# Sums of weight blocks: two of four by accumulating DMAs in place of VectorE

## The chip, the cores and the metric

The kernel runs on one core of one Trainium2 chip. The metric is the device time of one execution in microseconds (us); before the change the median of three runs is 703.41 us (703.22 to 703.43). All trace times below count from the start of the profiled span.

## The reference

One transformer layer on 2048 tokens of width 448, in float32:

```python
h  = x + fnet(layernorm(x))          # fnet: Real(DFT over tokens of DFT over width)
h2 = h + geglu(layernorm(h))         # (gelu(xn @ w_gate) * (xn @ w_up)) @ w_down, inner width 1792

# fnet:
a = einsum("bsd,ed->bse", x, dft_hid_re);  b = einsum("bsd,ed->bse", x, dft_hid_im)
y = einsum("ts,bse->bte", dft_seq_re, a) - einsum("ts,bse->bte", dft_seq_im, b)
```

The DFT matrices are inputs: those over tokens, 2048 x 2048 real and imaginary, are together the large operand W of the first stage.

## The kernel before, in words

The kernel applies W to the normalised x first (the sequence stage, to about 340 us) and the small DFT over the width after it, row block by row block. Gate, up and down projections follow. Every float32 operand is split into a high and a low float16 part (`hi_part`, L108, on ScalarE; `lo_part`, L112 and L114, on VectorE), and every product is three matmuls: high by high, high by low, low by high (`TERMS`).

The sequence stage is a loop over 64 units of W, `for n in range(N_STEPS)`. A unit is eight blocks of 128 x 128. Units 0 to 39 are multiplied block by block (`seq_mm`, L637). From unit `FAST` = 40 on, four units make one pass that uses products of Strassen's kind: for each pair of 2 x 2 blocks seven products (`PRODUCTS`) in place of eight. They need, beside the raw blocks A11, A12 and A22, four sums of the unit's blocks, S1 to S4 (`FORMS`), and sums of x's halves (T1 to T4, made by `t_load`, `t_norm`, `t_sums`, `t_hi` and `t_lo`). The matmuls are `fast_mm` (L509), 42 to a unit: two inner blocks i, seven products, three terms. A pass's seven sums in PSUM are combined by `fast_out` (L538, L541) into `zs`, which DMA transposes turn (`z_turn`, L658); the products with the small DFT are `hid_mm` (L719).

A unit n from 40 on goes through these steps:

- `seq_load(n)`: two DMAs on SP's queue (L421), one for each i, bring four blocks each (2 KB a partition) into the tile `wr`.
- `fast_sums(n)`: VectorE writes the four sums into a tile `sums`. L460 makes two of them in one instruction (blocks 1 and 2, each plus block 3, 512 elements a partition), L461 and L462 one each of 256 elements.
- `fast_raw(n)`: high and low part of the three raw blocks (768 elements).
- `fast_split(n)`: high part of the sums, two instructions of 512 elements on ScalarE, and low part, one instruction of 1024 elements on VectorE.
- `fast_mm(n, ...)`: the matmuls.

The order is written out by hand: each engine runs its instructions in the order of the program text, and SP its DMAs likewise. At step n, unit n is multiplied while unit n + 2 is prepared; after `fast_split` of unit n + 2 the load of unit n + 4 is issued. `fast_at` holds the steps of the first units (36, 38, 39, then 41 on). In the last unit of each pass (n % 4 == 3) `fast_raw` and `fast_split` come between the pieces of `fast_out`. The lists `early` and `after` place the other work of a step: loads, transposes, stores and splits of the gate and up weights (`Weights`), layer norm sums, hidden products. All DMAs are issued by SP; POOL does nothing between 1.4 us and 337.8 us.

`wr` and `sums` share a ring of five slots (tag `wr`); a slot is given out again when its tile's last reader is done, the one that came free first being the next. The inputs of `t_sums` lie in another ring, tag `xt`, of three slots.

Of the kernel before, what the change touches and what calls it, by code (L numbers as in the profile page):

```python
# [9 lines left out]
F32 = mybir.dt.float32  # L10
AF = mybir.ActivationFunctionType
ALU = mybir.AluOpType

P = 128
# [12 lines left out]
D_SC = 64.0  # L27
# [5 lines left out]
def kernel(  # L33
# [39 lines left out]
    nc = tc.nc  # L73
    V, A, G, PE = nc.vector, nc.scalar, nc.gpsimd, nc.tensor
# [32 lines left out]
    def hi_part(dst, src, scale=1.0):  # L107
        A.activation(dst, src, AF.Copy, scale=scale)  # L108

    def lo_part(dst, src, hi, scale=1.0):  # L110
        if isinstance(scale, float) and scale == 1.0:
            V.tensor_sub(dst, src, hi)  # L112
        else:
            V.scalar_tensor_tensor(dst, src, scale, hi, op0=ALU.mult, op1=ALU.subtract)  # L114
# [187 lines left out]
    dft = seq.enter_context(tc.tile_pool(name="dft", bufs=1, side="right"))  # L302
# [51 lines left out]
    xt, xs, norm_x = {}, {}, {}  # L354
# [51 lines left out]
    wr, ws = {}, {}  # L406

    def step_of(n):

        k, qq = divmod(n - NT, 4)  # L410
        return 2 + k // 2, k % 2, qq

    def seq_load(n):
        wr[n] = dft.tile([P, 8 * P], F32, tag="wr", bufs=5, name=f"wr{n}")
        if n < NT:
            nc.sync.dma_start(wr[n].rearrange("p (b t) -> p b t", b=4), w_seq[8 * (n % 2) + n // 2])
            return
        p, part, qq = step_of(n)
        for i in range(2):
            dst = wr[n][:, i * 4 * P : (i + 1) * 4 * P].rearrange("p (g t) -> p g t", g=2)  # L420
            nc.sync.dma_start(dst, w_seq[8 * p + 2 * qq + i][:, 2 * part : 2 * part + 2, :])  # L421
# [19 lines left out]
    FAST = N_STEPS - 24  # L441
    A_RAW = ("A12", "A11", "A22")
    FORMS = ("S3", "S1", "S2", "S4")
    T_OPS = ("T1", "T3", "T4", "T2")
    PRODUCTS = ("A11", "B11"), ("A12", "B21"), ("S2", "T2"), ("S3", "T3"), ("S1", "T1"), ("S4", "B22"), ("A22", "T4")
    fast_w, fast_s, fast_t, fast_acc, fast_e = {}, {}, {}, {}, {}

    def fast_views(n):
        raw = wr[n].rearrange("p (i b t) -> p i b t", i=2, b=4)
        s = fast_s[n].rearrange("p (s i t) -> p s i t", s=4, i=2)  # L450
        src = raw[:, :, 0:3].rearrange("p i b t -> p i (b t)")
        dst = fast_w[n][0][:, :, : 6 * P].rearrange("p l (i b) -> p l i b", i=2)
        return raw, s, src, dst

    def fast_sums(n):
        fast_s[n] = dft.tile([P, 8 * P], F32, tag="wr", bufs=5, name=f"sums{n}")
        fast_w[n] = [fast_tile(n, k, **place) for k, place in enumerate(fast_places(n))]
        raw, s, src, dst = fast_views(n)
        by_block = raw.rearrange("p i b t -> p b i t")
        V.tensor_add(s[:, 0:2], by_block[:, 1:3], by_block[:, 3:4].to_broadcast([P, 2, 2, P]))  # L460
        V.tensor_add(s[:, 2], s[:, 1], raw[:, :, 1])  # L461
        V.tensor_add(s[:, 3], raw[:, :, 0], s[:, 2])  # L462

    def fast_tile(n, k, pool=None, **place):
        return (pool or dft).tile([P, 2, 8 * P], F16, **place, name=f"ws{n}_{k}")

    def fast_places(n):
        ring = dict(tag="ws", bufs=6)
        return (dict(tag="raw", bufs=2, pool=prep), ring) if n == FAST + 2 else (ring, ring)

    def fast_raw(n):

        raw, s, src, dst = fast_views(n)
        hi_part(dst[:, 0], src, D_SC)
        lo_part(dst[:, 1], src, dst[:, 0], D_SC)

    def fast_split(n):

        w = fast_w[n][1]
        for part in slice(0, 4 * P), slice(4 * P, 8 * P):  # L480
            hi_part(w[:, 0, part], fast_s[n][:, part], D_SC)
        lo_part(w[:, 1], fast_s[n], w[:, 0], D_SC)

    def fast_a(n, i, l, name):
        if name in FORMS:
            k = 2 * FORMS.index(name) + i
            return fast_w[n][1][:, l, k * P : (k + 1) * P]
        k = 3 * i + A_RAW.index(name)
        return fast_w[n][0][:, l, k * P : (k + 1) * P]
# [14 lines left out]
    def fast_mm(n, i, k):  # L504

        j = 2 * (n % 4) + i
        a, b = PRODUCTS[k]
        for m, (lw, lx) in enumerate(TERMS):
            PE.matmul(  # L509
                fast_sum(n, k),  # L510
                fast_a(n, i, lw, a),
                fast_b(j, lx, b),
                start=j == 0 and m == 0 and k % 2 == 0,
                stop=j == NT // 2 - 1 and m == 2,
                skip_group_check=True,
            )
# [249 lines left out]
    for p, (n, half) in enumerate(turns):  # L766
        b, j = divmod(p, 2)
# [39 lines left out]
    for n in range(2, 5):  # L807
        seq_load(n)
# [27 lines left out]
    for n in range(N_STEPS):  # L836
# [10 lines left out]
        if n + 3 < FAST:  # L847
            seq_load(n + 5)
# [13 lines left out]
        if n in fast_at:  # L862
            unit = fast_at.index(n) + FAST
            fast_sums(unit)

            if n < FAST or n % 4 < 3:
                fast_raw(unit)
                fast_split(unit)
                if unit + 2 < N_STEPS:
                    seq_load(unit + 2)  # L870
# [7 lines left out]
        if n >= FAST:  # L878

            last = n % 4 == 3  # L880
            one = [(i, k) for k in range(7) for i in range(2)] if last else [(i, k) for i in range(2) for k in range(7)]
            if n % 4 == 0 and n > FAST:

                ks = (4, 5, 2, 3, 0, 1) if n == N_STEPS - 4 else range(6)
                one = [(i, k) for i in range(2) for k in ks] + [(i, 6) for i in range(2)]
            for m, (i, k) in enumerate(one):
                fast_mm(n, i, k)
                if last and i == 1 and k in (1, 3, 5, 6):  # L890
                    fast_out(n, k)
                    if n < N_STEPS - 1:
                        unit = n + 2
                        if k == 1:
                            fast_raw(unit)
                        elif k == 3:
                            fast_split(unit)
                            if unit + 2 < N_STEPS:
                                seq_load(unit + 2)
                if m in (6, 13):  # L900
                    for what in after.get((n, m // 7), ()):
                        what()
            continue
# [11 lines left out]
        else:  # L915
            p, part, qq = step_of(n)
# [392 lines left out]
    for t in range(NF):  # L1309
        w = gu.get(t + 2) if t + 2 in JIT_F else None  # L1310
        n = PREP_AT.get(t)
# [90 lines left out]
    for t in range(NF, N_GU):  # L1402
        now, ahead = steps[t], steps.get(t + 1, [])
# [36 lines left out]
        if ends:  # L1440
            p = now[-1] // NC
# [21 lines left out]
        for p, t0 in ended.items():  # L1463
            each = 3 if p < 3 else 2
            n = each * (t - t0)
# [106 lines left out]
```

## Time and profile before

| | |
|---|---|
| Median of three runs | 703.41 us |
| Profiled execution: its time, its span | 703.2 us, 701.1 us |
| TensorE busy | 696.3 us (99% of the span), clock 1.00 |
| VectorE, ScalarE, POOL busy | 551.0, 400.0, 95.4 us |
| Matmuls of the seven-product passes (L509) | from 219.2 to 339.9 us, 1008 of them |
| VectorE's sums, L460, L461, L462 | 24 times 684, 425 and 425 ns (medians) |
| DMA | 161.29 MB, queue of SP 76.0% of 16 engines |

The profile lists, for each engine, how long it was busy, and for each group of instructions its source line, what it writes and reads, its count, its busy time and what ended the idle time before it. The chain of waits follows the last instruction back through whatever released it; a stage in which the chain is all TensorE without gaps is one in which nothing made TensorE wait. The trace also gives single instructions in order of time (start, duration, engine, line), and busy times in stretches of the span.

### The profile page before, as it was taken

Reading aid. Unit: us, or ns where it says so; the run is one execution under the profiler, and the core shown is the slowest. Engines: PE = TensorE matmul, PEld = TensorE weight load, DVE = VectorE, ACT = ScalarE, POOL = GpSimd, SP = SyncE. Lnnn points to the kernel's source line nnn. Section 1 sums busy time; section 2 is a strip of 40 time slices with the busy share of each in tenths; the row PEclk is TensorE's granted clock in tenths of the full one; section 3 lists DMA queues with packets and bytes.
Section 4 is the critical chain, followed back from the end, with each engine's and each line's share of the span. In section 5 each row is a group of like instructions: output and inputs, shape, how many; then the busy total and the mean of one; then the engine's idle time right before and its main releaser. Section 6 shows DMA issues by size and latency. Waiting matters only on the chain.

```text
span 701.1 us, 13638 instructions
## 1 busy us (share of the span) xinstructions
PE 696.3 (99%) x5164; PEld 500.6 (71%) x5164; DVE 551.0 (79%) x1187; ACT 400.0 (57%) x787; POOL 95.4 (14%) x88
## 2 busy tenths in 40 slices
PE   9999999999999999999999999999999999999998
PEld 5555555555557889997644444469999999999997
DVE  7998667786798999986547798767777867899786
ACT  5876556666676566564526666555555453655631
POOL 0000000000000000000223333311020111232224
PEclk9999999999999999999999999999999999999999
DMA  8798578999997487384836878797879985877612
GB/s 276 252 255 303 121 267 227 334 288 289 269 287 195 141 195 200 117 205 179 233 125 212 288 242 236 189 326 231 245 209 326 247 299 170 318 274 276 239 39 79
DMA packets 116321, 161.29 MB, mean 230 GB/s; under 512 B 61984, under 2 KB 80544, under 8 KB 116256
## 3 DMA queue, kind: packets, MB, share of 16 engines
q1 hardware_dynamic: 116256, 160.43, 76.0%
q8 instruction: 40, 0.66, 0.4%
q14 instruction: 25, 0.20, 0.1%
HBM read 112.16 MB, written 34.34 MB: 209 GB/s over the span
## 4 chain that ended last, share of the span: by engine, by line
PE 98%; issue 1%; DMA 0%; DVE 0%; ACT 0%
PE acc L637 26%; PE acc_d L1232 15%; PE pY L1028 15%; PE acc_f L509 14%; PE pZ L1028 10%; PE pX L1028 10%; PE y L719 9%; DMA x<-in_x_dram 0%; ACT dn_w L108 0%; ACT v L958 0%; DVE st_x L122 0%; DVE xs L149 0%; DVE hr L1508 0%; ACT sd_x L129 0%; DVE r_x L373 0%
## 5 line engine op out<-in xcount | busy, mean ns | idle before, releaser
L637 PE MATMUL acc<-xs,ws 128*128 128x448 f16 x960 | 183.1, 352 | 0.1
L1028 PEld LDWEIGHTS <-gw 128*128 128x128 f16 x1443 | 140.9, 98 | 51.6
L637 PEld LDWEIGHTS <-ws 128*128 128x128 f16 x960 | 93.9, 98 | 87.7 <-DVE ws L114 0.2
L1232 PE MATMUL acc_d<-wd,dn_w 128*128 128x224 f16 x1008 | 110.6, 259 | 0.0
L1232 PEld LDWEIGHTS <-dn_w 128*128 128x128 f16 x1008 | 97.0, 98 | 1.9
L1028 PE MATMUL pY<-hops,gw 128*128 128x256 f16 (+1 forms) x629 | 98.1, 298 | 0.0
L509 PEld LDWEIGHTS <-ws 128*128 128x128 f16 x1008 | 96.6, 98 | 1.3
L1122 POOL TENSOR_TENSOR hs<-hs,c 128x256 f32<-128x256 f32 (+1 forms) x42 | 59.5, 1417 | 247.6 <-ACT c L1120 185.3
L114 DVE SCALAR_TENSOR_TENSOR ws<-wr,ws 128x1024 f16<-128x1024 f32 (+2 forms) x66 | 72.0, 1092 | 20.8 <-ACT ws L108 16.3
L108 ACT ACTIVATE ws<-wr 128x1024 f16<-128x1024 f32 (+2 forms) x66 | 61.9, 941 | 13.4 <-DMA wr<-in_w_seq_dram 8.0
L509 PE MATMUL acc_f<-t,ws 128*128 128x224 f16 x576 | 68.2, 259 | 0.0
L1028 PE MATMUL pZ<-hops,gw 128*128 128x256 f16 (+1 forms) x407 | 67.1, 298 | 0.0
L1028 PE MATMUL pX<-hops,gw 128*128 128x256 f16 (+1 forms) x407 | 67.1, 298 | 0.0
L719 PE MATMUL y<-wh,z 128*128 128x448 f16 x336 | 66.2, 352 | 0.0
L1073 ACT ACTIVATE pY<-pX 128x256 f32<-128x256 f32 (+1 forms) x42 | 18.4, 439 | 66.3 <-PE pX L1028 63.0
L215 POOL TENSOR_TENSOR wd_s<-wd 128x448 f32<-128x448 f32 x7 | 9.7, 1390 | 337.1 <-DVE e L538 336.3
L509 PE MATMUL acc_f<-xs,ws 128*128 128x224 f16 x432 | 55.1, 259 | 0.0
L719 PEld LDWEIGHTS <-z 128*128 128x128 f16 x336 | 32.9, 98 | 29.7
L1038 DVE SCALAR_TENSOR_TENSOR c<-pZ,u 128x256 f32<-128x256 f32 (+1 forms) x42 | 21.4, 510 | 38.8 <-PE pZ L1028 22.8
L1084 ACT ACTIVATE u<-pY 128x256 f32<-128x256 f32 (+1 forms) x42 | 19.1, 454 | 53.5 <-PE pY L1028 53.4
L112 DVE TENSOR_TENSOR dn_w<-dn_s,dn_w 128x640 f16<-128x640 f32 x48 | 41.5, 865 | 1.5 <-ACT dn_w L108 1.4
L108 ACT ACTIVATE dn_w<-dn_s 128x640 f16<-128x640 f32 x48 | 34.9, 728 | 12.1 <-DVE dn_s L1194 12.0
(144 smaller groups left out, 909.5 us busy)
## 6 DMA issues: line engine op xcount, KB each, us to landing
gw<-w_dram SPq DMA_DIRECT2D x37, 896.0 KB, 6.5
wr<-in_w_seq_dram SPq DMA_DIRECT2D x100, 256.0 KB, 4.6
hid_dram<-hs SPq DMA_DIRECT2D x27, 512.0 KB, 5.9
hid<-hid_dram SPq DMA_DIRECT2D x54, 256.0 KB, 5.8
w_dram<-gu_w SPq DMA_DIRECT2D x14, 896.0 KB, 6.5
gu_raw<-in_w_gu_dram SPq DMA_DIRECT2D x28, 384.0 KB, 6.1
wr<-in_w_seq_dram SPq DMA_DIRECT2D x14, 512.0 KB, 5.2
x<-in_x_dram SPq DMA_DIRECT2D x16, 224.0 KB, 3.1
```

The lines of the kernel that those rows point to most:

```text
L108: A.activation(dst, src, AF.Copy, scale=scale)
L112: V.tensor_sub(dst, src, hi)
L114: V.scalar_tensor_tensor(dst, src, scale, hi, op0=ALU.mult, op1=ALU.subtract)
L509: PE.matmul(fast_sum(n, k), fast_a(n, i, lw, a), fast_b(j, lx, b), start=j == 0 and m == 0 and k % 2 == 0, stop=j == NT // 2 - 1 and m == ...
L637: PE.matmul(acc[key][:, :D], w[:, lw, block * P : (block + 1) * P], xs[c][:, lx, :], start=c == 0 and m == 0, stop=c == NT - 1 and m == 2,)
L719: PE.matmul(y[:, :D], z[p][:, lz, k, g * P : (g + 1) * P], wh[:, lw, k, :], start=p == NP - 1 and k == 0 and m == 0, stop=k == 6 and m == ...
L1028: PE.matmul(ps, w[:, wl, wa + ws, :], ops[:, m + ms, :], start=first and n == 0, stop=last and n == len(terms) - 1, skip_group_check=True,)
L1038: V.scalar_tensor_tensor(dst, ps, SC, other, op0=ALU.mult, op1=ALU.add)
L1073: A.activation(self.Y, self.X, AF.Copy)
L1084: A.activation(self.u2, self.Y, AF.Copy, scale=SC)
L1122: G.tensor_mul(c22, c22, self.cols(self.c12))
L1232: PE.matmul(ps, w[:, la, a, :], wd[n][:, lb, b, :], start=n == 0 and m == 0 and opens, stop=n == NC - 1 and m == 2, skip_group_check=True,)
```

## The change

For units from 40 on the load is a function of its own. W's tile holds three raw blocks for each i in place of four. Beside it a tile of the same ring, shared by two units, receives blocks 1 and 2 by two plain DMAs on SP; then two DMAs issued by POOL add block 3, read from DRAM twice over by a broadcast access pattern, onto both. These two sums are thus ready when the second pair of DMAs has landed. `fast_sums` makes the other two on VectorE, 256 elements each, into a tile of the ring `xt`. `fast_split` and `fast_a` follow the new layout: the low part of the sums is two instructions of 512 elements.

```diff
     def seq_load(n):
+        if n >= FAST:
+            fast_load(n)
+            return
...
+    def fast_load(n):
+        p, part, qq = step_of(n)
+        wr[n] = dft.tile([P, 2, 3 * P], F32, tag="wr", bufs=5, name=f"wr{n}")
+        if n % 2 == 0:
+            pair["now"] = dft.tile([P, 2, 2, 2, P], F32, tag="wr", bufs=5, name=f"sums{n}")
+        fast_s[n] = pair["now"][:, n % 2]
+        blocks = [w_seq[8 * p + 2 * qq + i].rearrange("p g t -> p (g t)")[:, 4 * part * P :] for i in range(2)]
+        for i in range(2):
+            nc.sync.dma_start(fast_s[n][:, i], blocks[i][:, P : 3 * P].rearrange("p (s t) -> p s t", s=2))
+        for i in range(2):
+            nc.sync.dma_start(wr[n][:, i], blocks[i][:, 0 : 3 * P])
+        for i in range(2):
+            G.dma_start(
+                fast_s[n][:, i],
+                blocks[i][:, None, 3 * P : 4 * P].to_broadcast([P, 2, P]),
+                accum_op=ALU.add,
+            )
...
     def fast_sums(n):
-        fast_s[n] = dft.tile([P, 8 * P], F32, tag="wr", bufs=5, name=f"sums{n}")
         fast_w[n] = [fast_tile(n, k, **place) for k, place in enumerate(fast_places(n))]
-        raw, s, src, dst = fast_views(n)
-        by_block = raw.rearrange("p i b t -> p b i t")
-        V.tensor_add(s[:, 0:2], by_block[:, 1:3], by_block[:, 3:4].to_broadcast([P, 2, 2, P]))
-        V.tensor_add(s[:, 2], s[:, 1], raw[:, :, 1])
-        V.tensor_add(s[:, 3], raw[:, :, 0], s[:, 2])
+        t = dft.tile([P, 2, 2, P], F32, tag="xt", bufs=3, name=f"more{n}")
+        raw, sa = fast_views(n)[0], fast_s[n]
+        fast_s[n] = sa, t
+        V.tensor_add(t[:, :, 0], sa[:, :, 1], raw[:, :, 1])
+        V.tensor_add(t[:, :, 1], raw[:, :, 0], t[:, :, 0])
...
     def fast_split(n):
 
-        w = fast_w[n][1]
-        for part in slice(0, 4 * P), slice(4 * P, 8 * P):
-            hi_part(w[:, 0, part], fast_s[n][:, part], D_SC)
-        lo_part(w[:, 1], fast_s[n], w[:, 0], D_SC)
+        w = fast_w[n][1].rearrange("p l (h i s t) -> p l h i s t", h=2, i=2, s=2)
+        for h in range(2):
+            hi_part(w[:, 0, h], fast_s[n][h], D_SC)
+        for h in range(2):
+            lo_part(w[:, 1, h], fast_s[n][h], w[:, 0, h], D_SC)
```

More of the change, by code (lines that the diff above doesn't have):

```diff
@@ L445 @@
     PRODUCTS = ("A11", "B11"), ("A12", "B21"), ("S2", "T2"), ("S3", "T3"), ("S1", "T1"), ("S4", "B22"), ("A22", "T4")
-    fast_w, fast_s, fast_t, fast_acc, fast_e = {}, {}, {}, {}, {}
+    fast_w, fast_s, fast_t, fast_acc, fast_e, pair = {}, {}, {}, {}, {}, {}
+    def fast_load(n):
[15 more added lines that the diff above has]
+            )
     def fast_views(n):
-        raw = wr[n].rearrange("p (i b t) -> p i b t", i=2, b=4)
-        s = fast_s[n].rearrange("p (s i t) -> p s i t", s=4, i=2)
-        src = raw[:, :, 0:3].rearrange("p i b t -> p i (b t)")
+        src = wr[n]
+        raw = src.rearrange("p i (b t) -> p i b t", b=3)
         dst = fast_w[n][0][:, :, : 6 * P].rearrange("p l (i b) -> p l i b", i=2)
-        return raw, s, src, dst
+        return raw, src, dst
     def fast_sums(n):
-        fast_s[n] = dft.tile([P, 8 * P], F32, tag="wr", bufs=5, name=f"sums{n}")
         fast_w[n] = [fast_tile(n, k, **place) for k, place in enumerate(fast_places(n))]
-        raw, s, src, dst = fast_views(n)
-        by_block = raw.rearrange("p i b t -> p b i t")
-        V.tensor_add(s[:, 0:2], by_block[:, 1:3], by_block[:, 3:4].to_broadcast([P, 2, 2, P]))
-        V.tensor_add(s[:, 2], s[:, 1], raw[:, :, 1])
-        V.tensor_add(s[:, 3], raw[:, :, 0], s[:, 2])
+        t = dft.tile([P, 2, 2, P], F32, tag="xt", bufs=3, name=f"more{n}")
[3 more added lines that the diff above has]
+        V.tensor_add(t[:, :, 1], raw[:, :, 0], t[:, :, 0])
     def fast_tile(n, k, pool=None, **place):
@@ L471, in fast_raw @@
     def fast_raw(n):
-        raw, s, src, dst = fast_views(n)
+        raw, src, dst = fast_views(n)
         hi_part(dst[:, 0], src, D_SC)
@@ L477, in fast_split @@
     def fast_split(n):
-        w = fast_w[n][1]
-        for part in slice(0, 4 * P), slice(4 * P, 8 * P):
-            hi_part(w[:, 0, part], fast_s[n][:, part], D_SC)
-        lo_part(w[:, 1], fast_s[n], w[:, 0], D_SC)
+        w = fast_w[n][1].rearrange("p l (h i s t) -> p l h i s t", h=2, i=2, s=2)
[3 more added lines that the diff above has]
+            lo_part(w[:, 1, h], fast_s[n][h], w[:, 0, h], D_SC)
     def fast_a(n, i, l, name):
         if name in FORMS:
-            k = 2 * FORMS.index(name) + i
+            f = FORMS.index(name)
+            k = f // 2 * 4 + 2 * i + f % 2
             return fast_w[n][1][:, l, k * P : (k + 1) * P]
```

## The prediction

> **What bounds the kernel now.** I read the page's parts 1 and 4 first, then the chain of waits in order of time over the stage of the change, then that stage in windows of 20 us.
>
> ```profile
> span 701.1 us, 13638 instructions
> ...
> PE 696.3 (99%) x5164; PEld 500.6 (71%) x5164; DVE 551.0 (79%) x1187; ACT 400.0 (57%) x787; POOL 95.4 (14%) x88
> ...
> PE 98%; issue 1%; DMA 0%; DVE 0%; ACT 0%
> ```
> ```profile
> 219.40 18.11 PE acc_f L509 x189
> 237.51 3.97 PE y L719 x21
> ...
> 331.79 8.05 PE acc_f L509 x84
> ```
> ```profile
> 219.00:240.00 21.00, 21.00 (x207) 19.58 (x204) 19.35 (x43) 11.57 (x21) 0.00 (x0) 1.00 0.71 182
> 240.00:260.00 20.00, 20.00 (x190) 18.15 (x189) 19.61 (x37) 12.88 (x25) 0.00 (x0) 1.00 0.68 147
> 260.00:280.00 20.00, 20.00 (x191) 18.10 (x189) 19.49 (x39) 12.86 (x25) 0.00 (x0) 1.00 0.79 206
> 280.00:300.00 20.00, 20.00 (x190) 18.11 (x189) 18.59 (x31) 11.57 (x22) 0.00 (x0) 1.00 0.39 129
> 300.00:320.00 20.00, 20.00 (x191) 18.14 (x189) 17.61 (x30) 10.92 (x21) 0.00 (x0) 1.00 0.75 195
> 320.00:340.00 20.00, 20.00 (x181) 17.14 (x180) 9.69 (x25) 8.95 (x21) 2.19 (x3) 1.00 0.64 223
> ```
>
> The windows give length, then busy time of PE, PEld, DVE, ACT and POOL, granted clock, DMA share, GB/s. TensorE is busy throughout the stage at a clock of 1.00. A matmul of a seven-product pass takes 18.11 / 189 = 0.0958 us, a unit of 42 takes 4.02 us. 24 units (96.6 us) and six groups of 21 for L719 (6 x 3.97 = 23.8 us) make 120.4 us, and the stage lasts from 219.40 to 331.79 + 8.05 = 339.84, also 120.4 us. So not one microsecond in it is a wait of TensorE. VectorE, at 19.35 to 19.61 us of 20 up to 280 us, is nearly full too, but nothing on the chain waits for it.
>
> **What the change takes from VectorE.**
>
> ```profile
> 233.46 0.69 DVE L460 TENSOR_TENSOR sums<-wr 128x512 f32<-128x512 f32 x1 [0.93 <-DMA wr<-in_w_seq_dram]
> 234.19 0.43 DVE L461 TENSOR_TENSOR sums<-sums,wr 128x256 f32<-128x256 f32 x1
> 234.65 0.43 DVE L462 TENSOR_TENSOR sums<-wr,sums 128x256 f32<-128x256 f32 x1
> 234.99 0.42 DVE L243 TENSOR_TENSOR tt<-xn_h 128x256 f32<-128x256 f32 x1
> ...
> 238.36 1.22 DVE L114 SCALAR_TENSOR_TENSOR ws<-sums,ws 128x1024 f16<-128x1024 f32 x1
> 239.49 1.40 DVE L538 SCALAR_TENSOR_TENSOR e<-acc_f,e 128x224 f32<-128x224 f32 x4
> ```
> ```profile
> L114 DVE SCALAR_TENSOR_TENSOR ws<-wr,ws x66: 681/1218/1227, 5.8 to 324.9; 128x1024 f16<-128x1024 f32 x38, 128x768 f16<-128x768 f32 x24, 128x512 f16<-128x512 f32 x4
> ```
>
> From start to start the three sums of a unit hold VectorE 234.99 - 233.46 = 1.53 us. What stays is two adds of 256 elements, 234.99 - 234.19 = 0.80 us: 0.73 us less. The low part of the sums becomes two instructions of 512 in place of one of 1024: the one holds the engine 239.49 - 238.36 = 1.13 us; one of 512 takes 0.681 us in the last row, some 0.6 from start to start, so the two take 0.07 more. Net 0.66 us a unit, 15.8 us over 24 units. On the path this is worth nothing: TensorE, busy 20.00 of 20.00 us, hides it. ScalarE's high parts keep their forms, two of 512 a unit.
>
> **What it adds.** A unit's two loads on SP become four (the two for the sums first), and two DMAs on POOL follow that wait for the sums' loads. VectorE's first add, which wanted a landed load only, now wants a landed accumulation. Behind the POOL waits stands nothing: POOL's own list of waits has one of 336 us there.
>
> ```profile
> POOL wd_s L215 <- DVE e L538: 336.3, 1, 336.3
> ```
>
> So the question is when the accumulations land, and which unit has the least room. Most units' loads lie many microseconds ahead of use; unit 45 (L460 at 233.46 above) is the one that already waited 0.93 us for its load, because its load stands on SP behind a store that waits for VectorE and behind four transposes:
>
> ```profile
> 220.73 0.33 SPq L351 DMA_DIRECT2D w_dram<-gu_w  x1
> 221.15 7.51 SPq L658 DMA_TRANSPOSE z<-zs  x4
> ```
> ```profile
> 228.70 2.01 SPq L421 DMA_DIRECT2D wr<-in_w_seq_dram  x4
> ```
>
> The room from there to TensorE: a unit's first matmuls on sums are its third product. In units 46, 47 and 48 those start at
>
> ```profile
> 247.94 1.03 PE L509 MATMUL acc_f<-t,ws 128*128 128x224 f16 x9
> ...
> 252.53 1.89 PE L509 MATMUL acc_f<-t,ws 128*128 128x224 f16 x18
> ...
> 255.99 1.03 PE L509 MATMUL acc_f<-t,ws 128*128 128x224 f16 x9
> ```
>
> and the third matmul of each, 0.19 us later, is the first that reads the low part. Below, the start of unit 46's sums, and the low part of each of the three:
>
> ```profile
> 242.08 0.69 DVE L460 TENSOR_TENSOR sums<-wr 128x512 f32<-128x512 f32 x1
> ...
> 244.47 1.22 DVE L114 SCALAR_TENSOR_TENSOR ws<-sums,ws 128x1024 f16<-128x1024 f32 x1
> ...
> 250.07 1.22 DVE L114 SCALAR_TENSOR_TENSOR ws<-sums,ws 128x1024 f16<-128x1024 f32 x1
> ...
> 253.59 1.22 DVE L114 SCALAR_TENSOR_TENSOR ws<-sums,ws 128x1024 f16<-128x1024 f32 x1
> ```
>
> Room: 248.13 - 245.69 = 2.4 us (46), 252.72 - 251.29 = 1.4 us (47), 256.18 - 254.81 = 1.4 us (48). VectorE has no gap between 233.46 and these, so a later start of unit 45's sums moves all of it, less 0.66 us for each unit prepared since: 1.3, 2.0 and 2.6 us. The start may slip by 3.7, 3.4 or 4.0 us: **3.4 us** is free, and each microsecond beyond is one of TensorE, paid once, since from then on all later units have that much more room.
>
> How long an accumulation takes no row shows. The nearest:
>
> ```profile
> wr<-in_w_seq_dram SPq DMA_DIRECT2D x100, 256.0 KB, 4.6
> ...
> out_dram<-hr SPq DMA_DIRECT2D x4, 112.0 KB, 1.7
> ```
> ```profile
> DMA to landing us min/median/max: 2.5/4.6/7.7
> ```
>
> Each moves 128 KB in pieces of 512 B. The 112 KB stores at the kernel's quiet end (1.7 us) are the lower bound; the longest of W's loads (7.7 us) is the upper one. I take the median, 4.6 us: the accumulation has half the bytes, but it reads its target as well, the second stands behind the first on POOL, and units 46 and 47 load in the same microseconds.
>
> The Trainium skill, "DMA: Bandwidth & Descriptors", section "Anatomy of one DMA — SWDGE (gpsimd) path", fits a DMA issued from GpSimd with about 2.0 us plus its bytes at 436 GB/s. By that an accumulation would be an estimated 2.3 us and the sum would show no stall, 703.2 us. The trace speaks against using it here: for 256 KB the same fit gives 2.6 us, and the loads of W have a median of 4.6 us.
>
> The same lateness hits earlier, at units 40 and 41, whose loads also land just as VectorE wants them. What it delays there is VectorE's low part of gu_w, for which SP's store at 220.73 waits, with the transposes and unit 45's load behind it.
>
> ```profile
> 200.55 0.69 DVE L460 TENSOR_TENSOR sums<-wr 128x512 f32<-128x512 f32 x1
> ...
> 214.81 1.16 DVE L112 TENSOR_TENSOR t<-tx,t 128x448 f16<-128x448 f32 x2 [1.60 <-ACT t L108]
> ...
> 219.41 1.29 DVE L114 SCALAR_TENSOR_TENSOR gu_w<-gu_s,gu_w 128x512 f16<-128x512 f32 x2
> ```
> ```profile
> 200.00:219.00 19.00, 19.00 (x102) 9.83 (x101) 15.88 (x28) 13.89 (x28) 0.00 (x0) 1.00 0.82 267
> ```
>
> VectorE's idle time from 200 to 219 us is 19.0 - 15.9 = 3.1 us and three units save 2.0: 5.1 us against 4.6, so 0 if all of it can be used; if the 1.60 us wait for ScalarE stays, some 1.1 to 1.6 us. I take 0.8 us.
>
> **The sum.** 4.6 + 0.8 - 3.4 = 2.0 us of stall at unit 47. Everything else at nothing: two more issues a unit on SP (unit 46's loads are issued by 228.70 + 2.01 us and, even at 7.7 us, land at 238.4, while its sums start at 242.08); the smaller ring of W's tiles, which frees a unit's slots as late as before or one split (1.2 us) later; the new tile in the ring of t's inputs. If that cover goes, it is a later load of one unit, priced as the accumulation is. On the profiled execution's 703.2 us (2.1 us around its span; 0.2 us under the median of the runs) that is **705.2 us**. With the bounds, 1.7 + 0 - 3.4 < 0 gives 703.2, and 7.7 + 1.6 - 3.4 = 5.9 gives 709.1.
>
> **Rivals.**
>
> *Hidden: 703.2 us.* The accumulations land within 3.4 us of the loads. For it: the 1.7 us row, and that the loads for the sums have half the bytes. Against it: DMA shares of 0.9 to 1.1 just then:
>
> ```profile
> 225.00:230.00 5.00, 5.00 (x55) 5.00 (x53) 4.62 (x9) 3.18 (x6) 0.00 (x0) 1.00 1.07 149
> 230.00:235.00 5.00, 5.00 (x55) 5.00 (x53) 3.97 (x8) 3.32 (x7) 0.00 (x0) 1.00 0.91 289
> ```
>
> This is the side "not slower". A gain proper is nearly excluded, for there is no stall to take away.
>
> *The DMA engines fill up: about 711 us.* A unit moves 896 KB in place of 512 KB, 9.4 MB more in all, 15.7 if the target's reading counts.
>
> ```profile
> q1 hardware_dynamic: 116256, 160.43, 76.0%
> ```
>
> 160.43 MB in 76.0% of 701.1 us is 301 GB/s at full share: 31 to 52 us of all engines on a mean share of 0.66 over 121 us, so 0.9 to 1.1. A slot of W's ring comes free every three units, 3 x 120.4 / 24 = 15.1 us; load (4.6), accumulation and preparation (some 3 us) must fit in it, so accumulations above 7.5 us decide. At 9 us each later unit loses (16.6 - 15.1) / 3 = 0.5 us, 8 us over the 16 units from 48 on. Against it: windows such as 280 to 300 us have a share of 0.39. The Trainium skill, "DMA: Bandwidth & Descriptors", section "Issuing engines are not separate DMA queues", states that DMAs issued from any engine run on the same 16 DMA engines; no run here shows a DMA of POOL's yet.
>
> *It does not do what it says: about 708 us.* If two units that share a tile of sums are ordered against each other as one tile, the odd unit's load waits on SP for the even unit's accumulation. Unit 41's load and all SP work behind it slip by up to 4 us, and with them the transposes and unit 45: 2.0 + 3 = 5 us. Against it: different parts of one tile are written separately elsewhere in this kernel.
>
> **How the numbers follow.** Forecast 0.42 (its own range 704 to 707), hidden 0.37, engines full 0.11, ordered as one tile 0.07, faster 0.03. A measurement of this kernel tells 0.2%, 1.4 us, from no change. Of the forecast's cases about 0.05 lie under that: faster 0.03, same 0.42, slower 0.55. The range, 702.9 to 710.5, takes in the hidden case, both bounds and part of the case with full engines.
>
> **What would show it.** In the changed profile: L460 gone and two adds of 256 in its place; VectorE's share of 240 to 280 us lower by about 0.66 us a unit; POOL issuing 48 accumulations; a wait of VectorE's first add for a DMA at units 40, 41 and 45; one gap of TensorE of about 2 us near 252 us and none elsewhere before 340 us. Wrong would be: no gap (accumulations under 3.4 us), gaps repeating every few units (full engines), or a gap in another stage.

## The result and the profile after

The changed kernel takes 724.41 us (median of four runs, 721.60 to 724.93) against 703.42 us (four runs, 703.22 to 703.53): a ratio of 1.029 [1.027, 1.031], 21.0 us slower. The forecast was 705.2 us and the range ended at 710.5. The profiled execution below is one of 721.6 us, 18.7 us longer in its span than the one before.

First the page of the changed kernel: busy times, queues, chain, and the two groups of instructions that are new.

```profile
span 719.8 us, 13839 instructions
...
PE 701.1 (97%) x5164; PEld 501.2 (70%) x5164; DVE 537.1 (75%) x1187; ACT 399.0 (55%) x787; POOL 154.4 (21%) x136
...
q1 hardware_dynamic: 123168, 163.58, 75.6%
q0 software_dynamic: 13056, 6.29, 7.7%
...
PE 73%; DMA 11%; DVE 6%; ACT 3%; SPq 3%; issue 3%; POOL 0%; DVEq 0%; POOLq 0%; ACTq 0%
...
L463 POOL DMA_DIRECT2D sums<-in_w_seq_dram x48 | 58.7, 1459 | 280.9 <-DMA sums<-in_w_seq_dram 247.6
...
L480 DVE TENSOR_TENSOR more<-sums,wr 128x256 f32<-128x256 f32 x24 | 10.1, 422 | 46.8 <-issue 19.7
```

VectorE got what it was to get, 537.1 us of work in place of 551.0. But the chain is 73% TensorE where it was 98%, with 11% of DMA. TensorE's idle time went from 701.1 - 696.3 = 4.8 us to 18.7 us, and its busy time rose by 4.8 us although it does the same 5164 matmuls. VectorE now stands idle 46.8 us ahead of its first add (L480), in eleven of the 24 units.

The stage in windows of 20 us, as the prediction showed it (length, busy time of PE, PEld, DVE, ACT, POOL, clock, DMA share, GB/s):

```profile
220.00:240.00 20.00, 19.99 (x200) 19.01 (x199) 15.78 (x35) 14.14 (x27) 5.58 (x5) 1.00 1.02 252
240.00:260.00 20.00, 14.74 (x121) 11.74 (x119) 14.43 (x35) 9.70 (x20) 9.03 (x8) 0.91 0.98 179
260.00:280.00 20.00, 19.89 (x187) 17.84 (x188) 13.34 (x27) 9.44 (x19) 7.32 (x6) 1.00 1.11 200
280.00:300.00 20.00, 16.23 (x131) 13.17 (x129) 11.62 (x28) 6.92 (x13) 7.95 (x7) 0.91 1.14 229
300.00:320.00 20.00, 18.91 (x176) 16.49 (x174) 18.90 (x36) 14.69 (x31) 11.61 (x10) 1.00 0.98 211
```

There are two bad windows, not one, each with a lower mean clock. VectorE, nearly full before (18.6 to 19.6 us of 20 from 240 to 300 us), now stands idle for 28 to 42% of that time. The DMA share, 0.39 to 0.79 before, is 0.98 to 1.14 in these windows.

TensorE in order of time, the matmuls that waited and the slow ones behind them:

```profile
247.72 1.28 PE L530 MATMUL acc_f<-t,ws 128*128 128x224 f16 x6 [3.74 <-DVE e L559]
...
254.76 0.56 PE L530 MATMUL acc_f<-xs,ws 128*128 128x224 f16 x4 [0.63 <-DVE ws L114]
...
255.97 0.84 PE L530 MATMUL acc_f<-t,ws 128*128 128x224 f16 x7 [0.46 <-DVE ws L114]
...
260.11 1.13 PE L530 MATMUL acc_f<-xs,ws 128*128 128x224 f16 x10 [0.52 <-DVE ws L114]
...
283.72 1.22 PE L530 MATMUL acc_f<-xs,ws 128*128 128x224 f16 x10 [3.31 <-DVE ws L114]
284.74 3.50 PE L530 MATMUL acc_f<-t,ws 128*128 128x224 f16 x18
```

Eighteen matmuls in 3.50 us are 0.19 us each, twice the 0.096 us of the kernel before. Windows laid exactly on the time behind each of the two long stalls show why:

```profile
247.10:250.50 3.40, 2.77 (x14) 1.87 (x13) 3.37 (x8) 0.00 (x0) 0.00 (x0) 0.50 0.51 89
...
284.64:288.04 3.40, 3.40 (x21) 2.78 (x19) 3.33 (x9) 2.31 (x6) 1.50 (x2) 0.50 1.08 363
```

The granted clock was 0.50 for 3.4 us, twice. TensorE was busy for 2.77 and 3.40 us of them, which at half the clock is 1.4 and 1.7 us of matmuls more: a stall of 3.7 us became one of more than 5.

Where the time went can be read from TensorE's products with the small DFT (L740, L719 before), which come in groups of 21. In the changed kernel the last six groups of the stage start at 238.41, 266.02, 291.24, 313.38, 333.45 and 345.36 us; before, they start at 237.35, 257.42, 277.50, 297.57, 317.64 and 327.65 us. They are 1.1, 8.6, 13.7, 15.8, 15.8 and 17.7 us later. So 1.1 us was lost up to 238 us (a gap of 0.67 us at 208.7 us among it), 7.5 us by the stalls from 244 us on, 7.2 us by those from 280 us on, and 1.9 us by a last one of 1.74 us at 343.6 us.

Now VectorE, whose waits are behind those of TensorE:

```profile
205.65 0.43 DVE L480 TENSOR_TENSOR more<-sums,wr 128x256 f32<-128x256 f32 x1 [5.54 <-DMA sums<-in_w_seq_dram]
...
214.95 0.42 DVE L480 TENSOR_TENSOR more<-sums,wr 128x256 f32<-128x256 f32 x1 [4.61 <-issue]
...
245.01 0.42 DVE L480 TENSOR_TENSOR more<-sums,wr 128x256 f32<-128x256 f32 x1 [8.53 <-DMA wr<-in_w_seq_dram]
...
247.28 0.38 DVE L559 SCALAR_TENSOR_TENSOR e<-acc_f,e 128x224 f32<-128x224 f32 x1
...
281.91 0.42 DVE L480 TENSOR_TENSOR more<-sums,wr 128x256 f32<-128x256 f32 x1 [6.22 <-issue]
```

Units 40, 41 and 45 wait, as forecast, and unit 51 at 281.91 us, which was not; nor were the waits of units 50, 53 and 59 to 63, of 1.1 to 6.2 us. Of the releasers only the first row names the accumulation; in the trace the second accumulation of the unit landed at 214.87, 244.93 and 281.83 us, some 0.1 us before each of the other three adds. The row of L559 shows who stands behind unit 45 on VectorE: the combination of the pass that has just ended, which was at 236.47 us before and is 10.8 us later. That is what TensorE waited for at 243.98 us, since the next pass needs those sums' place in PSUM.

How long an accumulation took, from its issue on POOL to landing (minimum, median, maximum): all 48, those issued from 243 to 256 us, and those from 264 to 275 us.

```profile
DMA to landing us min/median/max: 3.7/6.1/11.1
...
DMA to landing us min/median/max: 3.9/4.4/5.3
...
DMA to landing us min/median/max: 3.8/8.7/11.1
```

In the quiet stretch the median is 4.4 us. From 264 to 275 us it is 8.7 us, and there SP's queue has this; of the kernel before the row of the same four transposes stands first, and behind each the time from issue to landing of these four:

```profile
261.62 5.25 SPq L658 DMA_TRANSPOSE z<-zs  x4
...
DMA to landing us min/median/max: 3.0/3.5/4.6
```
```profile
265.82 1.07 SPq L459 DMA_DIRECT2D sums<-in_w_seq_dram  x2
...
270.50 11.80 SPq L679 DMA_TRANSPOSE z<-zs  x4
...
DMA to landing us min/median/max: 5.8/10.2/11.3
```

Accumulations and transposes that ran at the same time here both took two to three times as long (8.7 against 4.4 us, 10.2 against 3.5 us). From the landing of a unit's two loads for the sums to the landing of both accumulations it took 5.0 to 11.6 us (24 units, median 7.0). Thirteen units took 5.0 to 7.1 us. Eleven took 8.1 to 11.6 us: units 41, 42 and 63 beside a load or store of 896 KB, units 50 to 52, 60 and 61 beside transposes, and units 45, 53 and 59 for most of their time beside neither, but with the loads and accumulations of the next units right behind.

### The profile page after: what moved, and what is told of

Read it like the earlier page. It is cut to its first block, busy times and chain, and to the rows that moved or that the text cites. A ratio compares the mean times of both kernels' runs of the same rounds, so it can differ in the third digit from the quotient of the medians.

```text
span 719.8 us, 13839 instructions
## 1 busy us (share of the span) xinstructions
PE 701.1 (97%) x5164; PEld 501.2 (70%) x5164; DVE 537.1 (75%) x1187; ACT 399.0 (55%) x787; POOL 154.4 (21%) x136
## 3 DMA queue, kind: packets, MB, share of 16 engines
q1 hardware_dynamic: 123168, 163.58, 75.6%
q0 software_dynamic: 13056, 6.29, 7.7%
## 4 chain that ended last, share of the span: by engine, by line
PE 73%; DMA 11%; DVE 6%; ACT 3%; SPq 3%; issue 3%; POOL 0%; DVEq 0%; POOLq 0%; ACTq 0%
PE acc L658 19%; PE acc_d L1253 15%; PE pY L1049 14%; PE pX L1049 9%; PE pZ L1049 9%; DMA sums<-in_w_seq_dram 7%; PE y L740 5%; SPq L679 2%; DVE ws L114 2%; DMA wr<-in_w_seq_dram 2%; PE acc_f L530 1%; DMA tx<-in_x_dram 1%; DVE more L480 1%; DMA hx<-in_x_dram 1%; DMA z<-zs 1%
## 5 line engine op out<-in xcount | busy, mean ns | idle before, releaser
L463 POOL DMA_DIRECT2D sums<-in_w_seq_dram x48 | 58.7, 1459 | 280.9 <-DMA sums<-in_w_seq_dram 247.6
L530 PE MATMUL acc_f<-t,ws 128*128 128x224 f16 x576 | 71.4, 265 | 5.1 <-DVE e L559 3.7
L740 PE MATMUL y<-wh,z 128*128 128x448 f16 x336 | 66.2, 352 | 2.4 <-ACT y L721 2.4
L108 ACT ACTIVATE ws<-wr 128x1024 f16<-128x1024 f32 (+2 forms) x66 | 61.8, 940 | 10.7 <-DMA wr<-in_w_seq_dram 9.2
L740 PEld LDWEIGHTS <-z 128*128 128x128 f16 x336 | 32.8, 98 | 32.6 <-issue 3.0
L480 DVE TENSOR_TENSOR more<-sums,wr 128x256 f32<-128x256 f32 x24 | 10.1, 422 | 46.8 <-issue 19.7
```

The lines of the kernel that those rows point to most:

```text
L463: G.dma_start(fast_s[n][:, i], blocks[i][:, None, 3 * P : 4 * P].to_broadcast([P, 2, P]), accum_op=ALU.add,)
L530: PE.matmul(fast_sum(n, k), fast_a(n, i, lw, a), fast_b(j, lx, b), start=j == 0 and m == 0 and k % 2 == 0, stop=j == NT // 2 - 1 and m == ...
L740: PE.matmul(y[:, :D], z[p][:, lz, k, g * P : (g + 1) * P], wh[:, lw, k, :], start=p == NP - 1 and k == 0 and m == 0, stop=k == 6 and m == ...
```

## The experiments

Two theories stood against each other. *Late sums*: the accumulations run too long beside other transfers, and VectorE, ScalarE and TensorE wait for their results. *Traffic*: the added pieces fill the DMA engines, and everything that is loaded comes late, whoever reads the sums.

**Without the accumulations.** The two DMAs on POOL are left out, so S1 and S3 lack block 3.

```diff
-        for i in range(2):
-            G.dma_start(
-                fast_s[n][:, i],
-                blocks[i][:, None, 3 * P : 4 * P].to_broadcast([P, 2, P]),
-                accum_op=ALU.add,
-            )
```

> The accumulations are left out (block 3 isn't added to S1 and S3); four loads a unit on SP in the new sizes stay, as do VectorE's two adds. Both theories: 703.4 us within 0.3%. If the smaller loads or the smaller ring of W's tiles cost anything by themselves, it shows here: over 705 us.

Measured: 703.44 us, ratio 1.0000 [0.9991, 1.0009]. All 21 us come with the accumulations. Four loads a unit, the smaller ring, the new tile in the ring of t's inputs and the split low part cost nothing, and the 0.66 us a unit that VectorE saves gain nothing.

**The DMAs by themselves.** A kernel of DMAs only: each step waits for an addition on VectorE, then issues two DMAs of 128 KB, or other transfers with them.

```diff
+    def adds(n=2, **kw):
+        for i in range(n):
+            G.dma_start(acc[:, i], blocks[i][:, None, 3 * P : 4 * P].to_broadcast([P, 2, P]), **kw)
...
+        start(zsrc)
+        for g in range(2):
+            for l in range(2):
+                nc.sync.dma_start_transpose(zdst[:, l, :, g * P : (g + 1) * P], zsrc[:, g, l, :])
+        adds(2, **add)
```

> No transformer layer, a bench of DMAs alone: plain loads from SP, plain and accumulating DMAs from POOL in pieces of 512 B and 1 KB, then two accumulations beside a store of 896 KB, two loads of 256 KB, four transposes, and eight adds of VectorE. Late data through queueing: about 4 us from issue to landing alone, 8 to 10 us beside the store (pieces of 7 KB) or the transposes. Slow in themselves: 6 us or more alone. Blocked by VectorE: longer beside its adds than alone.

Issue to landing, in order: two plain ones on POOL, two accumulations alone, two beside a store of 896 KB, two beside two loads of 256 KB, two beside four transposes, two beside VectorE's additions of 1024 elements. The last row is POOL's own for the two alone.

```profile
DMA to landing us min/median/max: 2.9/2.9/2.9
...
DMA to landing us min/median/max: 3.3/3.6/3.8
...
DMA to landing us min/median/max: 3.3/4.7/6.0
...
DMA to landing us min/median/max: 5.3/5.6/6.0
...
DMA to landing us min/median/max: 3.4/4.2/5.1
...
DMA to landing us min/median/max: 3.4/3.7/4.0
...
29.23 2.42 POOL L107 DMA_DIRECT2D acc<-in_w_seq_dram  x2 [3.28 <-DVE acc L101]
```

Alone a pair takes from POOL's first issue at 29.23 to 33.77 us, 4.5 us, so the 4.6 us of the prediction fits idle DMA queues, by luck: it was the median of W's loads, of twice the size, in a busy kernel. With another transfer beside it, which SP starts 0.8 to 1.6 us later, that becomes 5.9 us (transposes) to 6.8 us (store), not the 8 to 10 us of one DMA that I had expected; beside VectorE's work it is 4.7 us, nearly the same. The four transposes took 5.68 us to issue beside one pair and 5.25 us alone. In the kernel three pairs, W's loads and the transposes meet, and no single pairing here reaches the 11 us seen there.

**Plain in place of accumulating.** The DMAs stay, but overwrite the sums' place with block 3.

```diff
                 blocks[i][:, None, 3 * P : 4 * P].to_broadcast([P, 2, P]),
-                accum_op=ALU.add,
             )
```

> The same DMAs on POOL, same sizes, same waits, but they write block 3 over the sums' tile in place of adding it. If the reading of the target is what makes them slow (the pieces of 512 B took 71 ns on the software queue in the changed kernel, 30 ns on SP's queue before), they land 2 us or so earlier, and the time is 708 to 714 us. If it is POOL's queue and its sharing of the 16 engines, hardly less than the changed kernel's 724 us.

Measured: 715.40 us, ratio 1.016 [1.014, 1.018]. From the page of this kernel, the queue of POOL's DMAs, and issue to landing:

```profile
q0 software_dynamic: 2304, 6.29, 3.1%
...
DMA to landing us min/median/max: 2.7/4.5/11.6
```

The same 6.29 MB went in 2304 packets in place of 13056, and in 22 us of all engines (3.1% of 714.0) in place of 55 (7.7% of 719.8). That is worth 9 of the 21 us. The time lies between the two that I had named. The other 12 us are there with plain DMAs too; that they are the wait behind the loads and the sharing with other transfers (11.6 us from issue to landing at worst) is read from the trace and not tested by itself.

**Accumulations that nobody reads.** Three kernels were to keep the traffic and take away the wait. In the first S1 and S3 are the raw blocks (block 3 is left out); in the second, in addition, POOL reads one element of each tile of sums after the split, so that it keeps its slot; in the third the accumulations go to a spare 1 KB in the tile of W, and S1 and S3 lack block 3.

```diff
-        raw, sa = fast_views(n)[0], fast_s[n]
+        raw = fast_views(n)[0]
+        sa = raw[:, :, 1:3]
```

> The 48 accumulations run as in the changed kernel, but nothing reads what they add to: the forms S1 and S3 are taken from the raw blocks 2 and 1 in W's own tile (so block 3 is left out of them). Theory late data: the traffic is harmless and only the wait for the accumulations costs, so about 703.5 us. Theory full engines: the extra 48 DMAs slow loads and transposes for everyone, so 712 us or more, with TensorE still waiting.

> As the first run with unread accumulations (S1 and S3 from the raw blocks, block 3 left out of them), but POOL reads one element of each sum's tile at the place of the split, so that the ring of W's tiles is given out in the changed kernel's order and SP doesn't wait for accumulations that have just been issued. Theory late data (only the wait for the sums costs): 703.5 to 705 us. Theory full engines (48 accumulations slow all loads and transposes): over 712 us.

```diff
+        whole = dft.tile([P, 8 * P], F32, tag="wr", bufs=5, name=f"wr{n}")
+        wr[n] = whole[:, 0 : 6 * P].rearrange("p (i t) -> p i t", i=2)
+        spare = whole[:, 6 * P : 8 * P].rearrange("p (s t) -> p s t", s=2)
...
+        G.tensor_copy(spare, fast_s[n][:, 1])
         for i in range(2):
             G.dma_start(
-                fast_s[n][:, i],
+                spare,
```

> The 48 accumulations run with the same sizes and pieces, each from the landing of the sums' loads on, but their target is a spare 1 KB a partition in the tile of W's raw blocks, which nothing reads; S1 and S3 stay blocks 1 and 2 without block 3. So all of the added traffic is there and nobody waits for it. If the 21 us come only from the sums being ready later (theory A), this takes what the kernel without accumulations took, 703.4 us, to 704.5, and TensorE has no gap before 340 us. If the traffic itself delays W's loads and the transposes (theory B), units come late all the same: 706 to 714 us, with VectorE waiting for loads in place of accumulations. Above 715 us the waiting for the sums would be no part of it at all.

Measured: 735.79 us (1.046 [1.044, 1.047]), 728.67 us (1.036 [1.031, 1.041]) and 741.98 us (1.054 [1.052, 1.056]). All three brought in a wait of their own, so they tell nothing of the theories. In the first, SP's list of waits:

```profile
SPq L461 <- DMA sums<-in_w_seq_dram: 40.3, 7, 7.4
...
SPq L459 <- DMA sums<-in_w_seq_dram: 21.4, 4, 9.4
```

A tile that nobody reads gives its slot away while accumulations still write to it, and SP, with all of W's loads behind, waits for them; in the second kernel, too, that wait is 37.1 us in 15 times. In the third the second accumulation adds to the same place as the first and has to wait for it, so that POOL needs some 6 us a unit, 24 x 6 = 144 us for a stage of 120. What they show in passing: in these kernels accumulations that stand in the way of SP's queue or of POOL cost more (735.8, 728.7 and 742.0 us) than those in the way of VectorE (724.4 us).

The fourth has less of that: one accumulation a unit, of 128 KB, into the spare place. SP's list of waits still has 18.0 us in 5 times for DMAs into W's tiles.

```diff
+        G.tensor_copy(spare, fast_s[n][:, 1])
+        G.dma_start(spare, blocks[0][:, None, 3 * P : 4 * P].to_broadcast([P, 2, P]), accum_op=ALU.add)
```

> One accumulation a unit of 128 KB, half of the changed kernel's, from the landing of the sums' loads on (after a copy on POOL), into a spare 1 KB a partition of the tile of W's raw blocks, which nothing reads; S1 and S3 stay blocks 1 and 2 without block 3. Unlike the run with two accumulations on the same spare place, where the second had to wait for the first and POOL needed some 6 us a unit (24 x 6 = 144 us, longer than the stage), nothing here waits for an accumulation but a slot of W's ring, some 15 us later. If the traffic costs nothing by itself and only the late sums do (theory A): 703.4 to 704.5 us, no gap of TensorE before 340 us. If the traffic delays loads and transposes by so much that units come late (theory B): 706 us or more; at half of the pieces up to half of the 21 us, 714.

Measured: 704.00 us, ratio 1.0010 [1.0001, 1.0019]. Two windows of this kernel:

```profile
260.00:280.00 20.00, 20.00 (x190) 18.14 (x189) 15.02 (x33) 11.11 (x22) 6.14 (x7) 1.00 1.21 235
280.00:300.00 20.00, 20.00 (x191) 18.08 (x190) 19.14 (x38) 11.51 (x23) 10.56 (x12) 1.00 0.97 237
```

A DMA share of 0.97 to 1.21, and TensorE without a gap in them (in the stage it has two, of 0.20 and 0.52 us, at 248.6 and 252.5 us): half of the traffic, with no sum waiting for it, costs 0.7 us. This is against *traffic* as the cause by itself. Whether the whole of it, unread, would cost more was not settled.

**Sooner, in larger pieces, and both.** If the sums are late, an earlier issue helps. Five units' loads and accumulations go one step sooner.

```diff
+    SOONER = {34: 40, 35: 41, 40: 45, 48: 53, 57: 62}
...
+        if n in (34, 35, 40):
+            seq_load(SOONER[n], True)
...
+                if n in (48, 57):
+                    seq_load(SOONER[n], True)
```

> The changed kernel, its output whole; only the loads of units 40, 41, 45, 53 and 62 (with their accumulations) are issued one step sooner, ahead of the transposes or the store that held them up on SP. Late data at these units: most of the loss comes back, 704 to 709 us, and the waits of VectorE's first add for an accumulation near 245 and 294 us are gone. Full engines: the same accumulations share the same engines, over 716 us.

In the other kernel a further input holds each block 3 twice side by side, so that an accumulation goes in pieces of 1 KB.

```diff
-                blocks[i][:, None, 3 * P : 4 * P].to_broadcast([P, 2, P]),
+                w_twice[2 * (n - FAST) + i].rearrange("p (s t) -> p s t", s=2),
```

> The changed kernel, its output whole; block 3 lies twice side by side in DRAM, so that the accumulations go in 24576 bytes' worth of pieces of 1 KB instead of 512 B: half as many pieces, the same bytes added. If the turns that small pieces take beside other queues' pieces make them late, they land 2 us sooner and the time is 710 to 716 us. If the bytes that are read, added and written back count, under 3 us are gained: 721 us or more.

> Two earlier edits together: the loads and accumulations of units 40, 41, 45, 53 and 62 one step sooner (714.6 us alone, 9.8 under the changed kernel) and accumulations in pieces of 1 KB (718.2 us alone, 6.2 under it). If each removes a loss of its own, they add up: 724.4 - 16.0 = 708.4 us, 706 to 710. If both remove the same loss (queueing of the accumulations behind each other and beside the transposes), the larger one is all that is left: 713 to 715 us. Under 706 us would mean that the sooner issue failed only because several units' pieces queued up, as in the 6.45 us gap of TensorE that was left at 293.6 us there.

Measured: sooner 714.61 us (1.014 [1.011, 1.017]), in 1 KB pieces 718.20 us (1.021 [1.020, 1.023]), both 711.03 us (1.011 [1.008, 1.014]). Each gain is there (9.8, 6.2 and 13.4 us), the last less than the sum of 16.0. None of the three times lies in a range that I had named for it: each is between the two, so part of the loss goes with an earlier issue and part with larger pieces, and neither takes all of it. Sooner alone left stalls of TensorE of 2.55 us at 248.6 us and of 6.45 us at 293.6 us; VectorE's row of the long one:

```profile
298.19 0.43 DVE L483 TENSOR_TENSOR more<-sums,wr 128x256 f32<-128x256 f32 x1 [8.76 <-DMA sums<-in_w_seq_dram]
```

There three units' accumulations (54 to 56) were issued within 5 us (289.4 to 294.3 us) and landed 7.7 to 8.9 us after their loads. With both edits the stalls before 260 us are gone; the longest that are left are at the transposes of z, which take 14.68 us to issue now that three pairs of accumulations run with them:

```profile
266.53 14.68 SPq L683 DMA_TRANSPOSE z<-zs  x4
```
```profile
273.69 1.13 PE L534 MATMUL acc_f<-xs,ws 128*128 128x224 f16 x10 [1.63 <-DVE ws L115]
...
281.46 0.56 PE L534 MATMUL acc_f<-xs,ws 128*128 128x224 f16 x4 [3.52 <-DVE ws L115]
```

**Some units back to VectorE.** Here W's tile holds four blocks, and in chosen units VectorE adds block 3, in place of the accumulation; first in units 40, 41 and 45, then in nine whose accumulations landed 7 to 12 us after their loads. Units 42, 50 and 61, with 10.7, 8.2 and 8.2 us, keep theirs.

```diff
+    fast_four, BY_V = {}, (40, 41, 45, 51, 52, 53, 59, 60, 63)
...
+        if n in BY_V:
+            V.tensor_add(sa, sa, fast_four[n][:, :, None, 3 * P : 4 * P].to_broadcast([P, 2, 2, P]))
```

> The changed kernel, its output whole, but in units 40, 41 and 45 VectorE adds block 3 in place of the accumulation (their tile holds four blocks again). My early chain (units 40 and 41 delay a store, the store delays unit 45's load, and unit 45 stalls TensorE): the stall near 244 us, its half-clock stretch and the small ones up to 260 us go, some 7 to 9 us; those near 280 and 344 us stay, so 714 to 718 us. If the early stalls only move later: 720 us or more.

> VectorE adds block 3 in place of the accumulations in nine units, 40, 41, 45, 51, 52, 53, 59, 60 and 63 (a tile with four blocks, one more add of 512 elements): those whose accumulations ran beside a store of 896 KB or the transposes of z in the changed kernel and took 7 to 12 us. The other 15 units keep theirs; the output is whole. If the loss comes from accumulations that queue with those transfers (theory A): 704 to 707 us, with at most one gap of TensorE over 1 us before 345 us. If every accumulation costs its share, whatever runs beside it (theory B): 703.4 + 21 x 15 / 24 = 716.5 us, 713 to 720. With three units so changed (40, 41, 45) the time was 719.2 us.

Measured: 719.17 us (1.023 [1.017, 1.028]) with three, 707.28 us (704.37 to 710.19; 1.007 [1.004, 1.010]) with nine, at the upper end of the 704 to 707 us of theory A. With three the stalls before 260 us went, and longer ones came at 285 us (3.44 us) and 338 us (7.84 us), so that the time missed the 714 to 718 us that I had expected. With nine, two windows, and issue to landing of the accumulations that stay:

```profile
240.00:260.00 20.00, 20.00 (x190) 18.10 (x189) 19.35 (x41) 14.28 (x28) 7.32 (x6) 1.00 0.99 193
...
280.00:300.00 20.00, 19.85 (x189) 17.86 (x188) 16.05 (x32) 10.96 (x21) 10.08 (x9) 1.00 1.02 207
...
DMA to landing us min/median/max: 3.8/5.8/7.4
```

17.1 of the 21.0 us are gone with nine units of 24 (14 to 20 us, going by the single runs), where a like share for each would have left 716.5 us. No accumulation takes longer than 7.4 us from issue to landing any more, and TensorE has one gap of 0.15 us in the stage. The profiled execution took 704.4 us; where the others, up to 710.2 us, lost more is not shown.

Together the runs speak for *late sums*: without the accumulations nothing is lost, half of them unread cost 0.7 us at a DMA share of 1, and taking nine of the late ones off VectorE's path gives most of the time back. What makes the sums later than the 4.5 us that a pair takes alone is in turn the sharing of the DMA engines with other transfers, 5.9 to 6.8 us beside one of them in the kernel of DMAs.

No version beat the kernel before, and none could by much: TensorE had no stall in this stage to take away.

## Why the prediction was wrong

**What held.** The kernel before is bound by TensorE, VectorE's saving is worth nothing, and every edit but the accumulations costs nothing (703.44 us without them). The first waits came at units 40, 41 and 45, with unit 45 the first that hurts TensorE by more than 0.7 us. SP waits only 0.7 us in all for DMAs into tiles of sums, so the units of a pair are not ordered as one tile.

**What failed.** Two terms of the sum were too small, 4.6 us where 6.7 us came on the path and 0.8 us where 4.9 us came; with them the first stall is 6.7 + 4.9 - 3.4 = 8.2 us in place of 2.0, and 7.5 us were lost there. And the step from this stall to the total failed: the sum has one stall, while the runs showed further ones, of another 9.1 us in the profiled execution.

**The term "4.6 us" for an accumulation.** Its bounds were 1.7 and 7.7. Alone a pair takes 4.5 us; in the kernel the median from the landing of the loads is 7.0 us, and 8 to 12 us in eleven units. At unit 45 it was 8.3 us, of which 1.7 were won back, since the smaller loads landed sooner: 6.7 us on the path. The store had landed by then (231.79 us) and so had the transposes (235.19 us); beside the accumulations (236.56 to 244.93 us) ran only the loads and accumulations of units 46 and 47. The prediction named these loads, but it took a median over all of W's loads for a transfer that shares the engines with two more units.

**The term "0.8 us" for SP's queue.** Measured: 4.9 us, from 228.70 to 233.58 us for the issue of unit 45's load. The path was right, but the working set one lateness for units 40 and 41 together against the 5.1 us that I had found free. Each unit waited for its own: 5.54 + 4.61 = 10.2 us, and the store that waits for VectorE came 225.90 - 220.73 = 5.2 us later. The two rows of SP in the changed kernel:

```profile
225.90 0.33 SPq L351 DMA_DIRECT2D w_dram<-gu_w  x1
...
233.58 1.05 SPq L459 DMA_DIRECT2D sums<-in_w_seq_dram  x2
```

**The free room, "3.4 us".** Unit 45's add came 245.01 - 233.46 = 11.6 us late. By my sum that makes 11.6 - 3.4 = 8.2 us of stall; TensorE lost 7.5 us up to 266 us, of which 3.74 + 0.63 + 0.46 + 0.52 = 5.4 us in gaps and 1.4 us by the clock (the rest lies mostly at the edges of the gaps, where the last matmul counts as busy for 0.26 us in place of 0.096). The room was about right, but the first victim was another: the combination of the ended pass (L559), queued on VectorE behind the waiting add. Its row in the kernel before, and that of the matmuls that want its place:

```profile
236.47 0.38 DVE L538 SCALAR_TENSOR_TENSOR e<-acc_f,e 128x224 f32<-128x224 f32 x1
```
```profile
242.76 0.74 PE L509 MATMUL acc_f<-t,ws 128*128 128x224 f16 x6
```

It was done at 236.47 + 0.38 = 236.85 us, and TensorE wanted its place at 242.76 us: 5.9 us of room against 10.8 us of delay. TensorE itself was 1.2 us late by then (243.98 us), which leaves the 3.7 us of the first gap.

**"Paid once, since from then on all later units have that much more room".** This failed worst. I had measured room for units 46 to 48 only. In the trace of before the loads of units 50 to 52 landed 6.2 to 7.0 us before their add, that of unit 53 only 1.2 us and that of unit 62 only 2.0 us, and a stall moves loads and uses alike, as the load of a unit is issued behind the split of the one two before. Accumulations of 8 to 12 us at the next transposes used that up, at 280.41 us. That nine such units carry 17 of the 21 us is shown. What causes the length is read from the traces and was not separated by a run: the bunch of three units was enough for 8 us (45 and 53, beside which neither transposes of z nor 896 KB ran), and the 10 to 12 us came mostly beside one of these.

**The clock.** It was in no term. It made two stalls, of 3.74 and 3.31 us, longer by 1.4 and 1.7 us.

**The rival "the DMA engines fill up"**, given 0.11, named the resource and the point from which it decides (7.5 us). Its traffic, 31 to 52 us of all engines, was measured as 55 us on POOL's queue and 11 us more on SP's (75.6% of 719.8 us against 76.0% of 701.1), and the share in the windows above, 0.98 to 1.14, is the 0.9 to 1.1 of its sum. But it expected a loss at every unit, 8 us in all; what came is stalls at the bunches. The rule that it cited from the Trainium skill, "DMA: Bandwidth & Descriptors", section "Issuing engines are not separate DMA queues", says that DMAs of all issuing engines run on the same 16 DMA engines and interleave. The trace agrees: from first issue to last landing a pair of accumulations took 4.5 us alone, in the kernel of DMAs, and 12.1 and 10.4 us (units 51 and 52 of the changed kernel) beside the transposes of z, which took longer themselves.

## What to carry to other kernels

Price a transfer that is put on the path not by the median of its like, but by what the order of the program runs beside it, and look up the room at each such place, up to the end of the stage. Count the lateness once for each transfer that is late, not once for all. List what stands on the waiting engine behind the wait: its first victim may be another piece of work than the one that the data is for. A stall of TensorE can cost more than its length: here those of 3.3 and 3.7 us cost 1.4 to 1.7 us more by the clock.

## What the runs showed of the hardware

- An accumulating DMA did not go in larger packets than its 512 B pieces: 13056 packets, 55 us of all 16 engines, 68 ns each (7.7% of 719.8 us, times 16, over 13056). The plain DMA with the same addresses went in 2304 packets and 22 us. Of the accumulating packets 12288 have 512 B and took 71 ns in the mean, where SP's plain packets of 512 B took 30 ns in the kernel before; those of 1 KB took 116 ns where SP's took 49 ns.
- One accumulating DMA of 128 KB held POOL 1.2 us (two in 2.42), and landed 3.3 us after its issue with nothing beside it.
- After stalls of TensorE of 3.74 and 3.31 us the granted clock was 0.50 for 3.4 us; after one of 1.74 us it was not. The length of a stall alone does not decide it: in the kernel with plain DMAs one of 1.96 us, with one of 0.46 us behind it, was followed by 3.4 us at 0.50, and in the kernel with the sooner loads one of 2.55 us was not. In every profile of the layer above the clock changes only at whole multiples of 3.41 us from the start of its record. Counted in these steps, and from full clock, it was halved after 17 steps in which TensorE idled for 1.94 to 3.41 us (2.50 us ahead of the second slow stretch of the changed kernel, 281.22 to 284.63 us; 2.42 us with plain DMAs) and never after one with up to 1.83 us; one step with 2.01 us left it at 1.00, and the 2.55 us were 1.27 and 1.28 us in two steps. The Trainium skill, "TensorE: Matmul & The Clock Gate", Part 1, "The HAM clock gate (the "warmup" mystery)", says that an idle window of about 3.4 us halves the clock and a busy one restores it. The traces agree with the length of the window; but a step that was idle for somewhat more than half was already enough here. Ends of matmuls are modelled in the profile, so the idle times are rough by some 0.2 us a gap.
